# Pooled attention into a top-1 mixture of experts: another opening, and V's chunks cut at other keys

## The chip, the core and the metric

The kernel runs on one core of one Trainium2 chip. The metric is the device time of one launch in microseconds (us). A core has five engines that work beside each other: PE (TensorE, matrix products and transposes), DVE (VectorE), ACT (ScalarE), POOL (GpSimd) and SP, which here only issues transfers (DMAs).

## What is computed

Inputs are q, k and v, each of 8 batches x 8 heads x 576 rows x 64, and the weights of a gate and of 8 experts. K and V are averaged over groups of 8 rows, so that 72 keys are left for each head. Then follows ordinary attention, and after it one expert for each token.

```python
k_p = k.reshape(B, H, 72, 8, D).mean(axis=3)      # same for v_p
scores = scale * np.matmul(q, k_p.transpose(0, 1, 3, 2))
attn = softmax(scores)
x = np.matmul(attn, v_p)                          # tokens: 4608 x 512
expert_idx = argmax(x @ w_gate)
y = relu(x @ w1[e]) @ w2[e]                       # e: the token's expert
out = gate_probability * y
```

## The kernel before

The kernel has two stages. The attention goes over 36 units of 128 tokens (`units`, the loop `for i in range(NU)`), nine for each pair of batches. After it, blocks of 256 sorted tokens go through the experts (`up` and `finish`). Every engine runs its instructions in the order in which the program writes them, so the order in the text is the order on the engine.

One unit does this on PE: `u_pt` turns the exponentials of its 8 x 72 = 576 columns (padded to 640) in five transposes of 128 (L492); `u_pv` multiplies them with the masked V (L519; L514 for the four units that join two half batches); between them `g_s` makes scores of later units in two stages (L468), `g_qt` turns q (L445), and now and then a batch's K (`k_pe`, L357 and L360), V (`v_pe`, L371 to L377) and gate products (`u_pe`, L393, L395) are prepared. `rank` (L624 on) counts the tokens of each expert for a group of four units; it waits for a chain of small VectorE steps (`away` L600, `best` L606, `onehot` L615). VectorE takes the row minimum (`g_min`, L478), ScalarE the exponentials (`g_exp`, L485), VectorE divides (`u_nrm`, L549 to L551).

The 576 pooled rows of V lie in five chunks of at most 128 partitions, head after head. Chunk c holds parts of up to three heads, from head `HS[c]` on; a mask `mk` (L145) sets the rows of other heads to zero, and `SLOTS[c]` says which of the three a product takes. So `u_pv` multiplies chunk by chunk with 146, 219, 219, 219 and 73 columns (73 for a head: 64 of V, 8 of the gate, 1 for the sum). The result lies in two banks of four heads each, so the third product is cut in two: six products, 876 columns. A product of 32-bit numbers is two instructions on PE.

From the second batch on, GpSimd pools K and V (`pool`, L327, L329, L330) while other units run; most of these steps wait for the reciprocal L550 of the unit before (`on_beat`). Three buffers `kv` take K and V in turn.

The opening stands ahead of the loop. SP issues the loads in this order: K of batch 0 in three parts, a half of q (half of its rows of every head), V of batch 0, the gate weights in five small parts, the other half of q, K of batch 1, half of q of batch 1, and later V of batch 1. Meanwhile VectorE makes constants and zeroes buffers, and PE makes 36 products of ones that nobody reads (L708, `WARM`). VectorE pools K (`pool_now`, L336 to L338), PE turns each chunk twice, once for the lower 64 partitions (L717) and once for the upper (L718), because the scores take two tokens' rows at once through `BD`, a block diagonal of K. Then come the four stages of scores of the first group (`now`, `g_s`, `g_min`, `g_exp`), V pooled in two parts, `v_pe`, `u_pe`, and V masked (`u_dve`, L401, L406). GpSimd pools K of batch 1 behind V of batch 0 (L743 holds it back) and V of batch 1 behind the masked V (L746).

Of the kernel before, what the change touches and what calls it, by code (L numbers as in the profile page):

```python
# [21 lines left out]
WARM = 36  # L22
CS = 78
UPAT = (33, 34, 35)
HS = (0, 1, 3, 5, 5)
SLOTS = ((0, 2), (0, 3), (0, 3), (0, 3), (2, 3))
# [3 lines left out]
def kernel(  # L30
# [89 lines left out]

    jp = st1[1].rearrange("p c x -> p (c x)")[:, 0:128].bitcast(I32)
# [5 lines left out]
    ones = consts.tile([128, 128], F16, name="ones")  # L127
    nc.vector.memset(ones, 1.0)
# [12 lines left out]
    for c in range(5):  # L141
        nc.gpsimd.iota(rows[:, c, :], pattern=[[-KP, 3]], base=128 * c - KP * HS[c], channel_multiplier=1,
                       allow_small_or_imprecise_dtypes=True)
# [24 lines left out]
    for j, x in enumerate((0.0, 3.0, 2.0, 0.0)):  # L168
        nc.vector.memset(ahead[:, j:j + 1], x)
        nc.vector.tensor_copy(lists[:, j], inds)  # L170
    rank0 = consts.tile([128, E], F32, name="rank0")
    nc.vector.tensor_scalar(rank0, inds, float(8 * SEG + 1), None, op0=OP.mult)
    nc.vector.memset(rank0[:, 0:1], -float(1 << 17))
# [16 lines left out]
    nc.vector.tensor_scalar(head, tv, 0.0, None, op0=OP.is_equal)  # L190
# [8 lines left out]
    kv0 = consts.tile([128, 5, POOL * D], F32, name="kv0")  # L199
# [5 lines left out]
    nc.vector.tensor_scalar(thr[0:1, :], thr[0:1, :], -1.0, None, op0=OP.add)  # L205
# [35 lines left out]
    def load_kv(b, src):  # L241
        dst = kv[(2 * b + (src is vf)) % 3]
        nc.sync.dma_start(dst[0:64, 4, :], src[b, 512:576, :])
        step = 2 if b == 0 else 4
        for c in range(4 - step, -1, -step):
            nc.sync.dma_start(dst[:, c:c + step, :],
                              src[b, 128 * c:128 * (c + step), :].rearrange("(c p) x -> p c x", p=128))

# [9 lines left out]
    def load_qh(b, r):  # L258
        nc.sync.dma_start(qt[b][:, :, r:r + 2, :],
                          q[b, :, 0:128 * NM, :].rearrange("h (p r) d -> p h r d", r=NM)[:, :, r:r + 2, :])  # L260

    load_kv(0, kf)
    load_qh(0, 0)
    load_kv(0, vf)
# [3 lines left out]
    load_qh(0, 2)  # L268
    load_kv(1, kf)
    load_qh(1, 0)  # L270

    nc.vector.memset(kv[0][64:128, 4, :], 0.0)
    for i in range(1, 3):
        nc.gpsimd.memset(kv[i][64:128, 4, :], 0.0)
    nc.vector.memset(BD[0], 0.0)
# [56 lines left out]
    def pool_now(src, dst, part):  # L332
        p1 = pbig[:, 0:1280].rearrange("p (c x) -> p c x", c=5)
        p2 = pbig[:, 1280:1920].rearrange("p (c x) -> p c x", c=5)
        c = (slice(2, 5), slice(0, 2))[part]
        nc.vector.tensor_tensor(p1[:, c], src[:, c, 0:4 * D], src[:, c, 4 * D:], op=OP.add)  # L336
        nc.vector.tensor_tensor(p2[:, c], p1[:, c, 0:2 * D], p1[:, c, 2 * D:], op=OP.add)
        nc.vector.tensor_tensor(dst[:, c], p2[:, c, 0:D], p2[:, c, D:], op=OP.add)  # L338
# [58 lines left out]
    def u_dve(b):  # L397
        pm, vp = KVS.pop(("pu", b)), KVS.pop(("vp", b))

        def gates():  # L400
            nc.vector.tensor_tensor(VB[b % 3][:, :, :, D:D + E], pm[:, 0:120].rearrange("p (c s e) -> p c s e", s=3, e=E),  # L401
                                    mk[:, :, :, None].to_broadcast([128, 5, 3, E]), op=OP.mult)

        def masked(lo, hi):
            n = hi - lo
            nc.vector.tensor_tensor(VB[b % 3][:, lo:hi, :, 0:D], vp[:, lo:hi, None, :].to_broadcast([128, n, 3, D]),  # L406
                                    mk[:, lo:hi, :, None].to_broadcast([128, n, 3, D]), op=OP.mult)
            if hi == 5:
                laid.add(b)

        def masked_low():
            masked(0, 3)

        def masked_high():
            masked(3, 5)

        fillers[0:0] = [(-1, False, f) for f in (gates, masked_low, masked_high)]
# [70 lines left out]
    def u_pt(i):  # L488
        p = pbuf[i % 4]
        pp = psA.tile([128, 1024], F32, name="pp")  # L490
        for c in range(5):
            nc.tensor.transpose(pp[:, c * 128:(c + 1) * 128], p[:, c * 128:(c + 1) * 128], ident)  # L492
        pt = work.tile([128, 640], F32, name="pt")
        nc.scalar.activation(pt, pp[:, 0:640], AF.Copy)  # L494
        PP_[i] = pt

    def u_pv(i):
        b, r = units[i]
        a = PP_.pop(i)
        assert {b, b + (r is None)} <= laid and all(m[2] > b + (r is None) for m in moves)  # L500
        po = psA.tile([128, 2, 512], F32, name="po")
        PO_[i] = po
        first = {}
        for c in range(5):
            h0, hend = HS[c] + SLOTS[c][0], HS[c] + SLOTS[c][1]
            while h0 < hend:
                half = h0 // 4
                h1 = min(hend, 4 * half + 4)
                sl = slice(h0 - HS[c], h1 - HS[c])
                cols = slice((h0 - 4 * half) * CW, (h1 - 4 * half) * CW)  # L510
                st = first.get(half, True)
                if r is None:
                    for s in range(2):
                        nc.tensor.matmul(po[64 * s:64 * s + 64, half, cols],  # L514
                                         a[:, c * 128 + 64 * s:c * 128 + 64 * s + 64],
                                         VB[(b + s) % 3][:, c, sl, 0:CW], start=st, stop=False,
                                         skip_group_check=True)
                else:
                    nc.tensor.matmul(po[:, half, cols], a[:, c * 128:(c + 1) * 128],  # L519
                                     VB[b % 3][:, c, sl, 0:CW], start=st, stop=False, skip_group_check=True)  # L520
                first[half] = False
                h0 = h1
# [13 lines left out]
    def u_nrm(i, also=None):  # L536
        gidx, u = GOF[i]
        gs = bounds[gidx][1]
        if u == 0:
            drain(gidx - 2)  # L540
            flush(99, gidx - (3 if i < 30 else 2))
            X = XR[:, i % 12:i % 12 + gs, :]
            L = work.tile([128, 6, E], F32, name="L", bufs=2)
            GRP[gidx] = (X, L)
        X, L = GRP[gidx]
        po = PO_.pop(i)
        pv = po[:, :, 0:4 * CW].rearrange("p a (h x) -> p a h x", x=CW)
# [27 lines left out]
    whole(running(0), cum[:, :, None])  # L575
# [121 lines left out]
    def now(G, j):  # L697
        g_s(G, j)
        g_min(G, j)
        g_exp(G, j)  # L700

    def pooled(n, b):
        KVS[n, b] = work.tile([128, 5, D], F32, name=n, bufs=2)
        return kv[(2 * b + (n == "vp")) % 3], KVS[n, b]

# [3 lines left out]
    src, kp = pooled("kp", 0)  # L709
    pool_now(src, kp, 0)  # L710
    pool_now(src, kp, 1)
    g_qt(0, 0)
    g_qt(0, 1)
    pm = psA.tile([128, 1024], F32, name="pp")
    for c in (4, 2, 3, 0, 1):
        n = 128 if c < 4 else 64
        nc.tensor.transpose(pm[0:64, c * 128:c * 128 + n], kp[0:n, c], ident[0:n, 0:n])  # L717
        nc.tensor.matmul(pm[64:128, c * 128:c * 128 + n], kp[0:n, c], ident[0:n, 0:n], start=True, stop=True)  # L718
    for s in range(2):
        nc.scalar.activation(half(0, s), pm[64 * s:64 * s + 64, 0:H * KP], AF.Copy, scale=-SC)  # L720
    src, vp = pooled("vp", 0)
    pool_now(src, vp, 0)
    now(0, 0)
    pool_now(src, vp, 1)
    g_s(0, 1)
    v_pe(0)
    v_act(0)
    g_min(0, 1)
    g_exp(0, 1)
    g_s(0, 2)  # L730
    g_min(0, 2)
    g_exp(0, 2)
    u_pe(0)
    g_s(0, 3)
    g_min(0, 3)
    g_exp(0, 3)
    u_dve(0)
    drain(0)
    load_kv(1, vf)
    load_qh(1, 2)  # L740
    load_kv(2, kf)
    load_ql(0)
    nc.gpsimd.tensor_tensor(spacer[:, 0:1], vp[0:1, 0, 0:1], zf[0:1], op=OP.add)  # L743
    pool_k(1, 0)
    pool_k(1, 1)
    nc.gpsimd.tensor_tensor(spacer[:, 0:1], VB[0][0:1, 0, 0, 0:1], zf[0:1], op=OP.add)  # L746
    pool_v(1, 0)
    pool_v(1, 1)
    g_qt(1, 0)
# [3 lines left out]
    g_min(1, 1)  # L753
    load_kv(2, vf)
# [17 lines left out]
    prep(1, (0, ""), (1, ""), (2, ""))  # L772
# [164 lines left out]
    for i in range(NU):  # L937
# [8 lines left out]
        u_pt(i)  # L946
# [353 lines left out]
```

## Time and profile before

| | us |
|---|---|
| median of 3 runs | 611.68 (611.6 to 613.2) |
| the profiled execution | 610.65 |
| its span, from the first to the last instruction | 608.6 |
| PE busy | 581.4 (96% of the span) |
| first `u_pt` of the loop | 28.20 |
| last `u_pt` of the loop | 187.96 |

The profiled execution spends 2.05 us outside its span. PE is busy nearly throughout; VectorE 50%, ScalarE 45%, GpSimd 43% over the whole span, and more than that during the attention.

### The profile page before, as it was taken

To read this page: it belongs to the slowest core of one execution; us is meant where nothing else is said; L and a number is where in the kernel's file an instruction comes from. 1 tells how busy PE (TensorE), PEld (TensorE's weight loads), DVE (VectorE), ACT (ScalarE), POOL (GpSimd) and SP (SyncE) were. 2 spreads that over 40 slices of the span, in tenths; PEclk is the share of its full clock that TensorE was granted. 3 is DMA by queue.
4 is the path that set the end of the run, shared out by engine and by line. 5 is a ranking of instruction groups with operands and counts; after the bars stand their busy time and mean duration, and the time that the engine had idled before them with its cause. 6 is when DMAs were issued, how large, how long until landed. Compare 5 with 4: busy or idle time off the path is not lost. (4 is left out here: it accounts for less than half of the span.)

```text
span 608.6 us, 15118 instructions
## 1 busy us (share of the span) xinstructions
PE 581.4 (96%) x4391; PEld 436.9 (72%) x4392; DVE 304.0 (50%) x618; ACT 274.8 (45%) x620; POOL 263.1 (43%) x476
## 2 busy tenths in 40 slices
PE   6799999999799999999999999999999999999994
PEld 4699999898799467667756766757767567667672
DVE  5357778879865645214623212273123722183683
ACT  1577687877662245214522212272222722172671
POOL 5675888789964514202321121313222221214265
PEclk9999999999799999999999999999999999999998
DMA  9996789973345795985592143328543192318320
GB/s 246 301 318 203 259 249 328 326 233 136 117 114 191 192 350 128 406 237 108 136 323 66 54 108 83 83 55 284 153 108 81 35 355 81 102 34 291 90 59 11
DMA packets 96256, 107.10 MB, mean 176 GB/s; under 512 B 54366, under 2 KB 64606, under 8 KB 96224
## 3 DMA queue, kind: packets, MB, share of 16 engines
q1 hardware_dynamic: 89584, 85.72, 48.9%
q0 software_dynamic: 6640, 20.99, 9.1%
q8 instruction: 16, 0.26, 0.2%
q14 instruction: 16, 0.13, 0.1%
HBM read 72.99 MB, written 23.37 MB: 158 GB/s over the span
## 5 line engine op out<-in xcount | busy, mean ns | idle before, releaser
L998 PEld LDWEIGHTS <-bd 128*128 128x128 f16 x936 | 91.2, 98 | 105.8 <-DVE bd L992 0.9
L992 DVE SCALAR_TENSOR_TENSOR bd<-ps,bd 128x512 f16<-128x512 f32 (+1 forms) x44 | 27.5, 630 | 144.1 <-ACT bd L988 144.0
L1208 POOL TENSOR_TENSOR spacer<-ql,iG 1x1 f32<-1x1 f32 x44 | 18.6, 422 | 162.8 <-ACT ql L1204 153.0
L485 ACT ACTIVATE both<-ps,nmx 128x72 f32<-128x72 f32 x288 | 69.8, 347 | 7.1 <-DVE nmx L478 7.0
L519 PE MATMUL po<-vb,pt 128*128 128x146 f32 (+2 forms) x384 | 61.1, 308 | 1.5 <-DVE both L551 1.3
L519 PEld LDWEIGHTS po<-vb,pt 128*128 128x128 f32 x384 | 57.5, 192 | 4.0 <-issue 1.7
L998 PE MATMUL po<-w,bd 128*128 128x512 f16 x264 | 59.2, 379 | 0.0
L998 PE MATMUL po<-kv,bd 128*128 128x512 f16 x264 | 58.8, 379 | 0.0
L1209 POOL DMA_INDIRECT out_dram<-ql,iG x44 | 47.1, 1071 | 22.0 <-issue 20.6
L988 ACT ACTIVATE bd<-ps 128x512 f16<-128x512 f32 (+1 forms) x44 | 23.8, 547 | 69.1 <-PE L924 55.5
L468 PE MATMUL ps<-bd,qT 128*128 128x144 f32 x256 | 47.5, 313 | 2.1 <-ACT bd L720 1.4
L998 PE MATMUL pq<-kv,bd 128*128 128x512 f16 x216 | 48.1, 379 | 0.0
L653 POOL DMA_INDIRECT x_by_expert<-both,rpos x36 | 36.3, 1009 | 23.1 <-DVE both L649 10.1
L327 POOL TENSOR_TENSOR st<-kv 128x1280 f32<-128x1280 f32 x14 | 40.6, 2897 | 12.1 <-DVE ri L550 9.6
L926 PE MATMUL ps<-kv,qt 128*128 128x256 f16 (+1 forms) x176 | 44.8, 263 | 0.9 <-DVE qt L113 0.9
L924 PE MATMUL ps<-kv,w 128*128 128x256 f16 (+1 forms) x176 | 43.1, 258 | 1.9 <-ACT kv L111 1.5
L924 PE MATMUL ps<-kv,qt 128*128 128x256 f16 (+1 forms) x176 | 44.8, 263 | 0.0
L925 PE MATMUL ps<-kv,qt 128*128 128x256 f16 (+1 forms) x176 | 44.8, 263 | 0.0
L494 ACT ACTIVATE pt<-pp 128x640 f32<-128x640 f32 x36 | 25.5, 708 | 41.8 <-PE pp L492 41.8
L926 PE MATMUL ps<-kv,w 128*128 128x256 f16 (+1 forms) x176 | 43.1, 258 | 0.0
L925 PE MATMUL ps<-kv,w 128*128 128x256 f16 (+1 forms) x176 | 43.1, 258 | 0.0
L998 PE MATMUL pq<-w,bd 128*128 128x512 f16 x192 | 42.7, 379 | 0.0
(236 smaller groups left out, 1284.4 us busy)
## 6 DMA issues: line engine op xcount, KB each, us to landing
st<-in_moe_w_dram SPq DMA_DIRECT2D x8, 2048.0 KB, 13.7
both<-in_moe_w_dram SPq DMA_DIRECT2D x6, 2048.0 KB, 12.7
vb<-x_by_expert SPq DMA_DIRECT2D x16, 578.0 KB, 4.4
kv<-in_k_dram SPq DMA_DIRECT2D x7, 1024.0 KB, 9.0
kv<-in_v_dram SPq DMA_DIRECT2D x7, 1024.0 KB, 11.4
qt<-in_q_dram SPq DMA_DIRECT2D x6, 1024.0 KB, 11.5
st<-in_moe_w_dram SPq DMA_DIRECT2D x4, 1024.0 KB, 7.1
qt<-in_q_dram SPq DMA_DIRECT2D x4, 512.0 KB, 7.1
```

Source lines behind the costliest of these rows:

```text
L327: on_beat(nc.gpsimd.tensor_tensor(t1, src[:, :, 0:4 * D], src[:, :, 4 * D:], op=OP.add))
L468: nc.tensor.matmul(ps[:, x * 2 * KP:(x + 1) * 2 * KP], t[:, h, :], BD[b % 3][:, :, h, :], start=True, stop=True)
L485: nc.scalar.activation(p[:, h * KP:(h + 1) * KP], ps[:, x * KP:(x + 1) * KP], AF.Exp, bias=nmx[:, x:x + 1], scale=-1.0)
L494: nc.scalar.activation(pt, pp[:, 0:640], AF.Copy)
L519: nc.tensor.matmul(po[:, half, cols], a[:, c * 128:(c + 1) * 128], VB[b % 3][:, c, sl, 0:CW], start=st, stop=False, skip_group_check=True)
L653: st = nc.gpsimd.indirect_dma_start(out=xs, out_offset=bass.IndirectOffsetOnAxis(ap=Z["pos"][:, u:u + 1], axis=0), in_=X[:, u, :], in_offs ...
L924: nc.tensor.matmul(dst, wh, xT[:, d, 0:n], start=(d == 0), stop=False)
L925: nc.tensor.matmul(dst, wh, xT[:, DC + d, 0:n], start=False, stop=False)
L926: nc.tensor.matmul(dst, wl, xT[:, d, 0:n], start=False, stop=(d == DC - 1))
L992: V.scalar_tensor_tensor(l, p, 0.0, h, op0=OP.max, op1=OP.subtract)
L998: nc.tensor.matmul(y, hT[x][:, f, 128 * j:128 * j + 128], W2[s][z][:, f, :], start=(half == x == z == f == 0), stop=(half == z == 1 and f ...
L1209: st = nc.gpsimd.indirect_dma_start(out=out, out_offset=bass.IndirectOffsetOnAxis(ap=iG[:, j:j + 1], axis=0), in_=ys[j], in_offset=None, b ...
```

## The change

- V's chunks begin at keys 0, 128, 216, 344 and 472 (`VK`) instead of every 128. Chunks overlap, the last holds 104 rows. With `HS` and `SLOTS` as in the diff the products have 146, 146, 146, 219 and 146 columns, and the result lies in one run of eight heads whose border between banks falls between heads 2 and 3: five products, 803 columns. V's loads become three transfers of 616 rows in place of two of 576. `masked` lays out two heads instead of three for the first three chunks.
- In the opening, pooled K is written twice side by side (`kp` with 2 x 64 columns), so that one transpose serves lower and upper partitions (`k_first`); pooling, turning and copying of K go in two parts (chunks 0 and 1, then 2 to 4). V goes in the same two parts.
- The first q is loaded by heads (four and four, all rows) ahead of V, the second q in one transfer.
- 68 unread products instead of 36. The ones are set first on VectorE; small constants move behind the opening (`constants`); one zeroing moves from VectorE to GpSimd.
- The first `u_pt` goes into the opening, K of batch 1 is turned behind the first `u_pv` instead of ahead of it, V's and the gate's steps of batch 1 one unit later.

```diff
-WARM = 36
+WARM = 68
-HS = (0, 1, 3, 5, 5)
-SLOTS = ((0, 2), (0, 3), (0, 3), (0, 3), (2, 3))
+VK = (0, 128, 216, 344, 472)
+HS = (0, 1, 3, 4, 5)
+SLOTS = ((0, 2), (0, 2), (0, 2), (0, 3), (1, 3))
+LEFT = 3
...
     def load_kv(b, src):
         dst = kv[(2 * b + (src is vf)) % 3]
-        nc.sync.dma_start(dst[0:64, 4, :], src[b, 512:576, :])
+        if src is vf:
+            for c in (0, 2):
+                nc.sync.dma_start(dst[:, c:c + 2, :],
+                                  src[b, VK[c]:VK[c] + 256, :].rearrange("(c p) x -> p c x", p=128))
+            nc.sync.dma_start(dst[0:S - VK[4], 4, :], src[b, VK[4]:S, :])
+            return
...
     load_kv(0, kf)
     load_qh(0, 0)
+    load_qh(0, 4)
     load_kv(0, vf)
...
-    load_qh(0, 2)
     load_kv(1, kf)
-    load_qh(1, 0)
-
-    nc.vector.memset(kv[0][64:128, 4, :], 0.0)
...
+    load_q(1)
+    nc.gpsimd.memset(BD[0], 0.0)
...
         for c in range(5):
-            nc.tensor.transpose(pp[:, c * 128:(c + 1) * 128], p[:, c * 128:(c + 1) * 128], ident)
+            nc.tensor.transpose(pp[:, c * 128:(c + 1) * 128], p[:, VK[c]:VK[c] + 128], ident)
...
+            sl = slice(*SLOTS[c])
+            h = HS[c] + SLOTS[c][0]
+            cols = slice(o0 + h * CW, o0 + (HS[c] + SLOTS[c][1]) * CW)
...
+                nc.tensor.matmul(po[:, cols], a[:, c * 128:(c + 1) * 128], VB[b % 3][:, c, sl, 0:CW],
+                                 start=h in (0, LEFT), stop=False, skip_group_check=True)
...
+    def k_first(cs):
+        for c in cs:
+            n = 128 if c < 4 else 64
+            nc.tensor.transpose(pm[:, c * 128:c * 128 + n], kp[0:n, c].rearrange("p a d -> p (a d)"), ident[0:n, 0:n])
+
+    def k_keep(s, lo, hi):
+        if s and lo:
+            nc.vector.tensor_scalar(half(0, s)[:, lo:hi], pm[64:128, lo:hi], -SC, None, op0=OP.mult)
+        else:
+            nc.scalar.activation(half(0, s)[:, lo:hi], pm[64 * s:64 * s + 64, lo:hi], AF.Copy, scale=-SC)
+
+    pool_now(kv[0], kp, slice(0, 2))
+    k_first((0, 1))
+    k_keep(0, 0, 256)
+    k_keep(1, 0, 256)
+    pool_now(kv[0], kp, slice(2, 5))
     g_qt(0, 0)
+    k_first((2, 3, 4))
+    k_keep(0, 256, 576)
+    k_keep(1, 256, 576)
     g_qt(0, 1)
     now(0, 0)
+    now(0, 1)
+    pool_now(kv[1], vp, slice(0, 2))
+    g_qt(1, 0)
+    gates, masked = u_dve(0)
+    now(0, 2)
+    masked(0, 2)
+    pool_now(kv[1], vp, slice(2, 5))
+    now(0, 3)
+    u_pt(0)
     v_pe(0)
     v_act(0)
     u_pe(0)
+    masked(2, 3)
+    masked(3, 5)
+    gates()
     load_kv(1, vf)
-    load_qh(1, 2)
     load_kv(2, kf)
     load_ql(0)
...
-    g_qt(1, 0)
     g_qt(1, 1)
     now(1, 0)
     g_s(1, 1)
     g_min(1, 1)
+    constants()
     load_kv(2, vf)
...
-    prep(1, (0, ""), (1, ""), (2, ""))
+    prep(1, (0, "2"), (2, ""), (3, ""))
...
-        u_pt(i)
+        if i:
+            u_pt(i)
```

## Rows read from the trace of the kernel before

**Rows 1.** The page, part 1: busy time, share and instructions of each engine.

```profile
PE 581.4 (96%) x4391; PEld 436.9 (72%) x4392; DVE 304.0 (50%) x618; ACT 274.8 (45%) x620; POOL 263.1 (43%) x476
```

**Rows 2.** Windows, opening: length, PE, PEld, DVE, ACT, POOL busy, clock, DMA share, GB/s.

```profile
5.70:9.00 3.30, 0.00 (x0) 0.00 (x0) 3.20 (x7) 0.00 (x0) 3.30 (x6) 1.00 1.06 275
```

**Rows 3.** Timeline, opening, PE: start, us, what; idle before and its releaser in brackets.

```profile
1.67 3.76 PEld L708 LDWEIGHTS <-ones 128*128 128x128 f16 x36 [1.35 <-DVE ones L128]
9.05 1.97 PE L445 MATMUL pq<-ident,qt 128*128 128x128 f32 x8 [3.35 <-DMA qt<-in_q_dram]
...
23.31 0.98 PEld L468 LDWEIGHTS ps<-bd,qT 128*128 128x128 f32 x4
...
32.18 1.76 PEld L519 LDWEIGHTS po<-vb,pt 128*128 128x128 f32 x12 [0.17 <-issue]
33.86 0.55 PEld L468 LDWEIGHTS ps<-bd,qT 128*128 128x128 f32 x4
```

**Rows 4.** DMA view of the first 40 us: GB/s in slices of 1 us.

```profile
GB/s 0 0 199 303 399 337 288 334 203 320 380 221 221 276 220 299 377 324 332 262 215 350 386 333 299 203 258 389 354 150 246 238 379 383 225 293 360 381 353 348
```

**Rows 5.** Timeline, opening, VectorE and ScalarE.

```profile
11.00 0.96 DVE L336 TENSOR_TENSOR st<-kv 128x768 f32<-128x768 f32 x1 [1.61 <-DMA kv<-in_v_dram]
18.79 0.96 ACT L485 ACTIVATE both<-ps,nmx 128x72 f32<-128x72 f32 x4 [1.91 <-DVE nmx L478]
20.06 0.45 DVE L478 TENSOR_REDUCE nmx<-ps 128x4 f32<-128x288 f32 x1
```

**Rows 6.** Timeline, GpSimd: pooling of batch 1's K and V and of batch 2's K.

```profile
20.37 2.88 POOL L327 TENSOR_TENSOR st<-kv 128x1280 f32<-128x1280 f32 x1
...
26.50 0.43 POOL L746 TENSOR_TENSOR spacer<-vb,zf 1x1 f32<-1x1 f32 x1 [0.69 <-DVE vb L406]
26.90 2.87 POOL L327 TENSOR_TENSOR st<-kv 128x1280 f32<-128x1280 f32 x1
...
36.88 0.86 POOL L330 TENSOR_TENSOR kp<-st 128x320 f32<-128x320 f32 x1
```

**Rows 7.** Timeline, PE, in the third unit: gate products, K of batch 2, next unit's scores.

```profile
40.44 0.53 PEld L393 LDWEIGHTS pq<-wgb,vT 128*128 128x128 f32 x4
42.99 0.44 PEld L357 LDWEIGHTS pq<-ident,kp 128*64 128x64 f32 x4
```

**Rows 8.** Timeline, PE, narrow windows inside one `u_pv`; each line begins with its first matmul.

```profile
37.15 0.53 PE L519 MATMUL po<-vb,pt 128*128 128x219 f32 x2
37.33 0.52 PE L519 MATMUL po<-vb,pt 128*128 128x219 f32 x3
37.52 0.51 PE L519 MATMUL po<-vb,pt 128*128 128x73 f32 x3
37.58 0.57 PE L519 MATMUL po<-vb,pt 128*128 128x73 f32 x3
```

**Rows 9.** Timeline, GpSimd, VectorE and PE around units 24 and 28.

```profile
141.41 0.19 PE L624 MATMUL pq<-oh,before 128*128 128x32 f16 x1 [1.24 <-DVE oh L615]
157.03 1.91 POOL L118 TENSOR_TENSOR kv<-st,swc 128x1024 f32<-128x1024 f32 x1
157.11 1.89 DVE L600 TENSOR_TENSOR ra<-L,rm 128x32 f32<-128x32 f32 x1
159.03 2.16 DVE L606 SCALAR_TENSOR_TENSOR req<-ra,down 128x32 f32<-128x32 f32 x1
161.69 0.18 PE L624 MATMUL pq<-oh,before 128*128 128x32 f16 x1 [3.36 <-DVE oh L615]
161.83 1.31 PE L468 MATMUL ps<-bd,qT 128*128 128x144 f32 x4
168.43 0.70 PE L468 MATMUL ps<-bd,qT 128*128 128x144 f32 x4
172.28 0.70 PE L468 MATMUL ps<-bd,qT 128*128 128x144 f32 x4
```

**Rows 10.** Windows of 5 us, columns as in rows 2: the stretch of that wait.

```profile
160.00:165.00 5.00, 3.31 (x19) 3.29 (x19) 3.63 (x10) 0.91 (x3) 4.81 (x5) 0.60 0.28 82
```

More of the change, by code (lines that the diff above doesn't have):

```diff
@@ L204, with constants @@
     nc.gpsimd.iota(thr, pattern=[[SEG, E]], base=0, channel_multiplier=BLK, allow_small_or_imprecise_dtypes=True)
-    nc.vector.tensor_scalar(thr[0:1, :], thr[0:1, :], -1.0, None, op0=OP.add)
+    def constants():
+        for j, x in enumerate((0.0, 3.0, 2.0, 0.0)):
+            nc.vector.memset(ahead[:, j:j + 1], x)
+            nc.vector.tensor_copy(lists[:, j], inds)
+        nc.vector.tensor_scalar(rank0, inds, float(8 * SEG + 1), None, op0=OP.mult)
+        nc.vector.memset(rank0[:, 0:1], -float(1 << 17))
+        nc.vector.tensor_scalar(head, tv, 0.0, None, op0=OP.is_equal)
+        nc.vector.tensor_scalar(thr[0:1, :], thr[0:1, :], -1.0, None, op0=OP.add)
+        whole(running(0), cum[:, :, None])
     loads = ctx.enter_context(tc.tile_pool(name="loads", bufs=1))
@@ L242, in load_kv @@
         dst = kv[(2 * b + (src is vf)) % 3]
[L243 removed]
+        if src is vf:
[4 more added lines that the diff above has]
+            return
         step = 2 if b == 0 else 4
[L245 removed]
+        for c in range(0, 4, step):
             nc.sync.dma_start(dst[:, c:c + step, :],
                               src[b, 128 * c:128 * (c + step), :].rearrange("(c p) x -> p c x", p=128))
+        nc.sync.dma_start(dst[0:64, 4, :], src[b, 512:576, :])
     def load_q(b):
@@ L415, in masked_high @@
             masked(3, 5)
+        if b == 0:
+            return gates, masked
         fillers[0:0] = [(-1, False, f) for f in (gates, masked_low, masked_high)]
@@ L500, in u_pv @@
         assert {b, b + (r is None)} <= laid and all(m[2] > b + (r is None) for m in moves)
-        po = psA.tile([128, 2, 512], F32, name="po")
-        PO_[i] = po
-        first = {}
+        po = psA.tile([128, 2, 512], F32, name="po").rearrange("p a x -> p (a x)")
+        o0 = 512 - LEFT * CW
+        PO_[i] = po[:, o0:o0 + H * CW]
         for c in range(5):
[L505 to L522, printed above, removed]
+            sl = slice(*SLOTS[c])
+            h = HS[c] + SLOTS[c][0]
+            cols = slice(o0 + h * CW, o0 + (HS[c] + SLOTS[c][1]) * CW)
+            if r is None:
+                for s in range(2):
+                    nc.tensor.matmul(po[64 * s:64 * s + 64, cols], a[:, c * 128 + 64 * s:c * 128 + 64 * s + 64],
+                                     VB[(b + s) % 3][:, c, sl, 0:CW], start=h in (0, LEFT), stop=False,
+                                     skip_group_check=True)
+            else:
+                nc.tensor.matmul(po[:, cols], a[:, c * 128:(c + 1) * 128], VB[b % 3][:, c, sl, 0:CW],
+                                 start=h in (0, LEFT), stop=False, skip_group_check=True)
     GRP = {}
@@ L713 @@
     g_qt(0, 1)
[L714 to L722, printed above, removed]
```

81 lines of the change are left out of this document (31 added, 50 removed).

## The prediction

> **What bounds the kernel now.** I read the page's busy times first, then the opening, then the places where PE waits. PE is busy 96% of the span [rows 1], so work taken from PE counts wherever nothing else is late. The exception is the opening. From 5.70 to 9.00 PE does nothing while the transfers run flat out [rows 2], then it waits 3.35 us for q [rows 3]. In the opening PE is also at the lower of its two clock levels, although the window's clock column reads 1.00. Four instructions of scores take 0.98 us at 23.31 and 0.55 us at 33.86 [rows 3]. 36 products of 128 columns take 3.76 us, 0.104 us each [rows 3], which is 128 columns at 1.2 GHz. So the spacing of like instructions is the witness here. The 36 products did not raise the clock in this execution; what came behind them still ran at half speed.
>
> In the attention PE runs dense, except that it waits at `rank` for VectorE. The worst wait is 3.36 us at 161.69 [rows 9]. There `away` (L600) and `best` (L606), which are small, take 1.89 and 2.16 us because GpSimd's L118 starts 0.08 us ahead of L600 and L119 follows. In that stretch the granted clock is 0.60 in the mean [rows 10], between the levels of 2.4 GHz (1.00) and 1.2 GHz (0.50): it fell after the idle time. And the next unit takes 168.43 - 161.83 = 6.60 us where the one after it takes 3.85 [rows 9].
>
> **Part 1, the opening.** I price it at one point, the turn of batch 2's K in the third unit, at 42.99 before [rows 7], because there GpSimd's pooling meets PE.
>
> Data first. I add up the slices of the DMA view [rows 4]. By 7.5 us 1.70 MB have come, which is K (1.18) and half of q (0.52); q was used at 9.05 [rows 3], a lag of 1.5. By 9.9 us 2.36 MB have come, which adds V's first parts; VectorE used them at 11.00 [rows 5], a lag of 1.1. I take 1.3. Behind the change the order is K 1.18, q 1.05, V 1.26 (616 rows of 2 KB), K of batch 1 1.18, q 1.05, V of batch 1 1.26, in all 6.98 MB against 6.29 up to the same V. The slices reach 6.98 MB at 25.5 us, so it lands near 26.8. q now moves in pieces of 1 KB instead of 512 bytes. If that removes the three weak slices (203, 221, 221), some 0.2 MB or 0.8 us are won: 26.0. At the best stretch's pace it would be 24.5.
>
> GpSimd pools that V from 26.90 and has batch 2's K at 36.88 + 0.86 = 37.74 [rows 6], so 10.84 us later. Before, its start hung on the masked V at 26.50 [rows 6]; now it hangs on the data. That chain gives 36.8 to 37.6, at best 35.3. So the faster opening buys GpSimd almost nothing; the wait for the masked V becomes a wait for a transfer.
>
> PE's own way there. The second half of q is complete at 2.23 MB, 9.5 + 1.3 = 10.8 us. The four stages of scores need 0.96 us of ScalarE each and a minimum of 0.45 [rows 5]. The last minimum stands on VectorE behind V's second pooling, whose data (3.49 MB) land at 14.0 + 1.3 = 15.3. Its first step alone is 0.96 [rows 5], the next two halve the columns, so some 1.8: 17.1. Then 0.45 and 0.96: 18.5. Between there and the first `u_pv` PE has 16 turns at 0.11 (0.44 for four [rows 7]), three stages of scores at 0.55 [rows 3] and the gate products (from 40.44 [rows 7] to the next product at 41.35: 0.9): 4.35 us at 2.4 GHz, twice that at 1.2, and some 2 us in which it waits for ScalarE's copies and exponentials. So the first `u_pv` begins between 24.9 and 29.2, against 32.18 [rows 3]. From there to the turn of batch 2's K took 42.99 - 32.18 = 10.8. The change puts 12 turns of batch 1's K in (1.3), takes the gate products out (0.9) and shortens three products (0.4): 10.8 again. That gives 35.7 to 40.0.
>
> The later of both ways counts: 37.2, the middle of GpSimd's chain, since PE's lower end is ahead of it. 42.99 - 37.2 = 5.8; before, the gate products of batch 1 were done by then (0.9), so **4.9 us** are won. Bounds: PE at 1.2 GHz throughout gives 2.1; the best pace of transfers gives 6.3. The single transpose in place of two, the constants moved behind (some 2 us of VectorE, in the way only of the second group's minimum) and the zeroing on GpSimd (1 us where GpSimd is idle for batch 0's data) I cost at nothing beyond this: the data cover them. If the data came at once, the turns would be worth about 2 us.
>
> The 68 products end, at 0.104 each from about 1.1 us on, at 8.2 us or sooner if the clock rises in between; the first pooled chunks are ready near 6.6. So they can delay the first turns by up to 1.6 us, but q's first half arrives at 8.8 anyway, and the delay is covered. Whether the clock, once up, lasts is open, since PE would then idle from about 14.6 to 18.5. After 3.4 us of idle it was down at 161.83; after 1.24 us at 141.41 nothing slowed [rows 9]. So I expect it down again by the first `u_pt`, which is why I don't take the lower end. The Trainium skill, TensorE: Matmul & The Clock Gate, Part 4 (PE-mode transpose), speaks against the change too: transposes, it says, don't count as busy for the clock. By that rule the turns behind the 68 products would not hold the clock, and the time would be that of the 1.2 GHz end, 2.8 us later. The half-speed turns from 9.05 on agree, but don't prove it.
>
> **Part 2, the products with V.** In one unit 876 columns take 33.86 - 32.18 = 1.68 us [rows 3] in 12 instructions. The change turns 2 x 146, 2 x 219, 2 x 73 into 4 x 146, 1 x 219, every product two instructions. By columns alone it saves 73 / 876 of 1.68 = 0.14. By spacing, 219 columns take 0.18 and 73 take 0.06 [rows 8], up to 0.11 where a heavier one follows; 146 take as long as the scores' 144, 0.55 / 4 = 0.138 [rows 3]. So the change is 2 x 0.18 + 4 x (0.06 to 0.11) - 4 x 0.138 = 0.05 to 0.25. I take **0.14**, inside both. 33 units behind the opening's point: 4.6 us. PE is dense there, so it lies on the path, save where PE waits for VectorE behind GpSimd: the wait of 1.24 us at 141.41 [rows 9] just grows by what units 22 to 24 save, 0.4. **4.2 us** remain (1.2 to 7.8). Two extra SP issues for each V and 7% more of V's bytes are behind work that is loaded units ahead: nothing. VectorE's shorter masks are off the path.
>
> **Sum.** 610.65 (span 608.6 and 2.05 around it) - 4.9 - 4.2 = 601.55. The median of the runs lies 1.03 above the profiled execution: **602.5**. The experts' stage only moves earlier.
>
> **Rivals.**
> - *The wait at 161.69 dissolves.* Without the lock L606 would begin at 157.11 + 0.25 + 0.03 = 157.39 (0.25 being my estimate of a free L600). Units 25 to 27 bring VectorE 3 x 0.14 = 0.42 forward, while GpSimd, which is all but never idle there (4.81 of 5 us [rows 10]), stays: 156.97, 0.06 ahead of L118 at 157.03. Then only `onehot` is caught, until 158.94, and PE goes on at 159.2 instead of 161.69, without the slow unit: 2.5 + 2.75 = 5.2 us. That gives 597.3. Against it: the margin is thinner than the scatter of one instruction. The Trainium skill, SBUF, names the lock: one pair of ports between VectorE and GpSimd, held for a whole instruction; 1.89 us for L600 against GpSimd's 1.91 agrees.
> - *The opening gives only its lower end, 2.1,* with PE slow from the idle time on: 605.3.
> - *The products don't shrink as their columns do,* at 0.05 a unit (weight loads or issue set the pace): 33 x 0.05 less the same 0.4 at unit 24: 605.5.
> - *Slower.* `rank` comes eight times, and only one wait now costs clock. New phases between VectorE and GpSimd could catch two more groups as at unit 28, at 3.36 + 2.75 = 6.1 us each: 602.5 + 12.2 = 614.7. It takes two; one gives 608.6. For it speaks that GpSimd leaves so few gaps [rows 10]; against it, that the earlier waits are 1.24 us or less and GpSimd's steps hang on the reciprocals, so the phases move together.
>
> **How the numbers follow.** Chances: forecast 0.42, dissolved wait 0.30, lower opening 0.11, small products 0.08, one more caught wait 0.04, slower 0.05. A measurement of this kernel tells about 0.3% (1.8 us) from no change. Faster 0.91, same 0.04, slower 0.05. The range 595.0 to 608.0 takes in the dissolved wait with a better opening and the weak openings with weak products.
>
> **What would show it.** GpSimd's L327 for V of batch 1 should begin at 26 to 27 behind a DMA, and K of batch 2 be turned near 37. L519 should be ten instructions in about 1.54 us. The wait at unit 28 should read 3 us or near 1. Wrong would be: GpSimd starting that V before 25 (transfers faster), the first `u_pv` behind 29, or `rank` waits above 3 us elsewhere.

## The result and the profile after

The changed kernel takes 604.29 us (median of 4 runs, 601.66 to 605.96), the kernel before 612.44 beside it; the ratio is 0.9865 with a 95% interval of 0.9837 to 0.9893. The forecast was 602.5 us with a range of 595.0 to 608.0. A repeat on another chip gave 600.87 (0.9832, 0.9799 to 0.9865). Why the two medians lie 3.4 us apart is open, but for one stall that is shown below. The execution profiled first is the slowest of its four: 605.96 us, span 603.7.

The page of after, part 1, against [rows 1]:

```profile
PE 571.7 (95%) x4333; PEld 426.4 (71%) x4334; DVE 301.5 (50%) x619; ACT 274.6 (45%) x621; POOL 265.5 (44%) x477
```

PE has 58 instructions fewer and 9.7 us less work; the span is 4.9 us shorter. PE stays the busiest engine, but it stands idle more. Where the time went is read off four marks, in us from the start of the span:

| mark | before | after | after, repeated |
|---|---|---|---|
| K of batch 2 turned (PEld) | 42.99 | 38.54 | 38.25 |
| last `u_pt` | 187.96 | 178.50 | 178.15 |
| second block of the experts | 210.25 | 204.81 | 200.22 |
| end | 608.6 | 603.7 | 599.1 |

So the opening gives 4.45, the attention 5.0 more, the passage to the experts takes 4.0 back in the first execution and nothing in the repeat, and the rest is as long as it was within 0.6 us.

The opening of after, PEld rows of the timeline (the last one stands against the last of [rows 7]):

```profile
1.07 5.88 PEld L712 LDWEIGHTS <-ones 128*128 128x128 f16 x68 [0.75 <-DVE ones L124]
25.77 2.74 PEld L531 LDWEIGHTS po<-vb,pt 128*128 128x128 f32 x10
38.54 0.45 PEld L371 LDWEIGHTS pq<-ident,kp 128*64 128x64 f32 x4
```

68 products at the pace of the 36 [rows 3], 0.104 us, would take 7.1 us; they take 5.88, so the clock rose inside them. It did not last. PE waited 2.2 us for exponentials before 17.04, and the windows (columns as in [rows 2]) show the granted clock at the lower level from 20 on:

```profile
20.00:24.00 4.00, 3.36 (x14) 2.96 (x14) 1.27 (x7) 1.59 (x6) 3.84 (x3) 0.50 1.07 344
24.00:28.00 4.00, 3.99 (x16) 3.96 (x17) 1.74 (x13) 2.35 (x9) 2.27 (x3) 0.50 1.09 262
28.00:33.00 5.00, 4.89 (x33) 4.04 (x32) 1.75 (x5) 2.24 (x6) 4.84 (x4) 0.86 1.12 277
```

The first `u_pv` at 25.77 therefore takes 2.74 us for its ten products, and PE is itself late at batch 2's K. GpSimd is as forecast: V of batch 1 begins at 26.70 behind a DMA, K of batch 2 is pooled at 36.72 + 0.86 = 37.58 (against [rows 6]):

```profile
26.70 2.89 POOL L338 TENSOR_TENSOR st<-kv 128x1280 f32<-128x1280 f32 x1 [1.73 <-DMA kv<-in_v_dram]
...
36.72 0.86 POOL L341 TENSOR_TENSOR kp<-st 128x320 f32<-128x320 f32 x1
```

A unit in the steady stretch, PE, first before, then after (one `u_pv` and the scores behind it):

```profile
63.18 1.91 PE L519 MATMUL po<-vb,pt 128*128 128x146 f32 x12
64.92 0.70 PE L468 MATMUL ps<-bd,qT 128*128 128x144 f32 x4
65.46 0.71 PE L492 MATMUL pp<-ident,both 128*128 128x128 f32 x5
```

```profile
41.87 1.64 PE L531 MATMUL po<-vb,pt 128*128 128x146 f32 x10
43.34 0.65 PE L485 MATMUL ps<-bd,qT 128*128 128x144 f32 x4
43.83 0.71 PE L509 MATMUL pp<-ident,both 128*128 128x128 f32 x5
```

From start to start `u_pv` takes 1.74 before and 1.47 after, the scores behind it 0.54 and 0.49: 0.32 us a unit. In narrow windows inside one `u_pv` of after the starts of the products of 146 columns (each line begins with the first matmul of its window) lie 0.125 us apart:

```profile
42.22 0.54 PE L531 MATMUL po<-vb,pt 128*128 128x146 f32 x3
42.35 0.54 PE L531 MATMUL po<-vb,pt 128*128 128x146 f32 x3
42.47 0.60 PE L531 MATMUL po<-vb,pt 128*128 128x146 f32 x3
42.60 0.47 PE L531 MATMUL po<-vb,pt 128*128 128x146 f32 x2
```

Before, the short products of 73 columns hold up what stands behind them. The first instruction of 146 columns behind such a pair takes 0.17 us to the next start:

```profile
64.08 0.65 PE L519 MATMUL po<-vb,pt 128*128 128x146 f32 x3
64.25 0.66 PE L519 MATMUL po<-vb,pt 128*128 128x146 f32 x3
```

The scores behind `u_pv`, which ended on such a pair, show the same: they took 0.54 and now take 0.49, or 0.12 for each instruction of 144 columns.

The other side of the account is `rank`. Before, PE waits there three times for `oh`, 4.8 us in all (the view of waits: total, times, longest); after, seven times:

```profile
PE pq L632 <- DVE oh L623: 7.8, 7, 2.2
```

Unit 24, where [rows 9] show 1.24 us, now looks as unit 28 did before (timeline of GpSimd, VectorE and PE):

```profile
129.53 1.90 POOL L120 TENSOR_TENSOR kv<-st,swc 128x1024 f32<-128x1024 f32 x1
131.51 2.12 POOL L121 TENSOR_TENSOR w<-kv,w 128x1024 f16<-128x1024 f32 x1
130.57 0.92 DVE L608 TENSOR_TENSOR ra<-L,rm 128x32 f32<-128x32 f32 x1
131.53 2.15 DVE L614 SCALAR_TENSOR_TENSOR req<-ra,down 128x32 f32<-128x32 f32 x1
134.18 0.19 PE L632 MATMUL pq<-oh,before 128*128 128x32 f16 x1 [2.19 <-DVE oh L623]
135.69 1.17 PE L485 MATMUL ps<-bd,qT 128*128 128x144 f32 x4
```

The window around it, its clock in the third column from the right:

```profile
130.00:140.00 10.00, 7.81 (x52) 7.08 (x51) 8.65 (x21) 6.28 (x25) 9.44 (x8) 0.83 0.48 160
```

GpSimd's L121 starts 0.02 us ahead of `best` (L614) and both end within 0.05 us of each other; PE loses 2.19 us and from 135.69 on runs scores at half pace. At unit 28 the wait is 1.99, in other executions up to 4.24.

The loss in the passage to the experts, in the first execution alone, in PE's timeline and in the window:

```profile
200.29 0.38 PE L1137 MATMUL pq<-ident,tf 128*8 128x128 f32 x1 [2.58 <-DVE tab L1134]
```

```profile
198.00:204.00 6.00, 3.71 (x11) 1.43 (x12) 2.67 (x9) 0.69 (x1) 4.10 (x10) 0.72 0.30 108
```

In each of the thirteen other profiled executions, the kernel before among them, PE waits 0.44 to 0.46 us at this turn. So nothing ties the 2.58 us to the change.

### The profile page after: what moved, and what is told of

It reads as the page before. It is cut to its first block, busy times and chain, and to the rows that moved or that the text cites. A ratio compares the mean times of both kernels' runs of the same rounds, so it can differ in the third digit from the quotient of the medians.

```text
span 603.7 us, 15016 instructions
## 1 busy us (share of the span) xinstructions
PE 571.7 (95%) x4333; PEld 426.4 (71%) x4334; DVE 301.5 (50%) x619; ACT 274.6 (45%) x621; POOL 265.5 (44%) x477
## 5 line engine op out<-in xcount | busy, mean ns | idle before, releaser
L1013 PE MATMUL po<-w,bd 128*128 128x512 f16 x264 | 60.5, 386 | 0.0
L531 PE MATMUL po<-vb,pt 128*128 128x146 f32 (+1 forms) x320 | 52.7, 311 | 1.8 <-ACT pt L511 1.8
L531 PEld LDWEIGHTS po<-vb,pt 128*128 128x128 f32 x320 | 47.1, 194 | 3.7 <-ACT pt L511 2.9
L485 PE MATMUL ps<-bd,qT 128*128 128x144 f32 x256 | 45.6, 304 | 1.4 <-ACT both L502 1.2
L338 POOL TENSOR_TENSOR st<-kv 128x1280 f32<-128x1280 f32 x14 | 40.6, 2903 | 11.8 <-DVE ri L559 7.1
```

Source lines behind the costliest of these rows:

```text
L338: on_beat(nc.gpsimd.tensor_tensor(t1, src[:, :, 0:4 * D], src[:, :, 4 * D:], op=OP.add))
L485: nc.tensor.matmul(ps[:, x * 2 * KP:(x + 1) * 2 * KP], t[:, h, :], BD[b % 3][:, :, h, :], start=True, stop=True)
L531: nc.tensor.matmul(po[:, cols], a[:, c * 128:(c + 1) * 128], VB[b % 3][:, c, sl, 0:CW], start=h in (0, LEFT), stop=False, skip_group_check ...
L1013: nc.tensor.matmul(y, hT[x][:, f, 128 * j:128 * j + 128], W2[s][z][:, f, :], start=(half == x == z == f == 0), stop=(half == z == 1 and f ...
```

## The experiments

The theory to be tested was that three things set the time: GpSimd's pooling sets the end of the opening, shorter products shorten each unit, and small steps of VectorE that stand beside GpSimd's long ones take part of it back. Marks are those of the table above, from one profiled execution each; each kernel also ran against the kernel before, on its own chip.

| kernel | median us (lowest to highest) | ratio to before | K of batch 2 | last `u_pt` | second block |
|---|---|---|---|---|---|
| again | 600.87 (600.55 to 601.44) | 0.9832 | 38.25 | 178.15 | 200.22 |
| opening_only | 609.69 (604.68 to 612.72) | 0.9987 | 37.16 | 181.65 | 203.86 |
| products_only | 606.51 (605.08 to 608.95) | 0.9930 | 40.65 | 178.77 | 200.90 |
| warm36 | 603.00 (601.63 to 603.55) | 0.9858 | 39.56 | 179.55 | 201.65 |
| rank_later | 607.29 (605.69 to 608.89) | 0.9938 | 38.50 | 185.79 | 207.86 |
| no_split | 592.30 (591.50 to 592.92) | 0.9696 | 38.29 | 168.98 | 191.11 |
| more_warm | 600.07 (599.17 to 600.31) | 0.9815 | 37.20 | 177.85 | 199.99 |
| split_quarters | 601.49 (599.52 to 602.88) | 0.9845 | 37.62 | 177.10 | 199.21 |
| opening_no_split | 603.22 (599.26 to 607.08) | 0.9861 | 39.08 | 177.43 | 199.70 |
| before_no_split | 603.91 (603.36 to 603.95) | 0.9874 | 44.25 | 181.22 | 203.56 |
| split_behind | 599.04 (597.62 to 600.63) | 0.9806 | 38.23 | 175.97 | 198.09 |
| split_pool_behind | 603.28 (601.87 to 604.89) | 0.9867 | 37.88 | 181.48 | 203.55 |

**The parts of the change, one at a time** (four kernels on one chip).

`again`, the changed kernel unaltered:

> The changed kernel once more, unaltered. Its first profile lost 4.0 us between the last turn of a unit and the second block of experts (a gain of 9.5 us at the one point, 5.4 at the other). If that loss belongs to the change, it is here again, with PE idle some 2.6 us ahead of the turn of the table. If it belongs to the one execution, the gain of some 9 us at the last unit reaches the end, and the time is nearer 602 than 606.

`opening_only`, the old products and chunks put back:

```diff
-VK = (0, 128, 216, 344, 472)
-HS = (0, 1, 3, 4, 5)
-SLOTS = ((0, 2), (0, 2), (0, 2), (0, 3), (1, 3))
-LEFT = 3
+VK = (0, 128, 256, 384, 512)
+HS = (0, 1, 3, 5, 5)
+SLOTS = ((0, 2), (0, 3), (0, 3), (0, 3), (2, 3))
...
```

> The changed kernel with the products of before: chunks every 128 keys, six products, 876 columns, two banks of four heads. My theory: opening and products add up, and the opening is worth what was won at the turn of batch 2's K, 42.99 - 38.54 less 0.9 of gate products = 3.5 us: about 609. Rival: the opening is the whole gain and the columns are hidden: about 604.

`products_only`, the kernel before with the new chunks and products alone:

> The kernel before with V's chunks at the new keys and five products of 803 columns (V in three transfers, first V in the old order), and the old opening. My theory: a unit's products fall from 1.68 to 1.48 us, 36 x 0.20 = 7.2 us, of which the waits at rank take back 1 to 3: 606 to 608. Rival: the columns are hidden behind VectorE or the transfers: 611 to 612.

`warm36`:

```diff
-WARM = 68
+WARM = 36
```

> The changed kernel with 36 unread products instead of 68. My theory: the clock stays at 1.2 GHz until some 30 us, so the first scores and turns run at half pace, but transfers and ScalarE set most of that stretch, and GpSimd has batch 2's K no earlier than 37.5 anyway: its turn comes 0 to 2 us later than 38.54, the time is 604 to 606. Rival: the raised clock makes the opening's gain: 607 to 608.

Measured up to the second block in the profiled executions, the opening alone gives 6.4 us, the products alone 9.35, both 10.0. They don't add up in these executions, and the waits at `rank` show where it goes. The view of waits, first of opening_only, then of products_only, then of again:

```profile
PE pq L639 <- DVE oh L630: 5.2, 4, 3.4
```

```profile
PE pq L626 <- DVE oh L617: 9.8, 7, 4.2
```

```profile
PE pq L632 <- DVE oh L623: 9.2, 7, 3.3
```

With the old products the waits are nearly the old ones; with the new products there are seven, with either opening. Of the 2.4 us by which again has K of batch 2 earlier than products_only, 0.9 are the gate products that stand behind the mark in again and ahead of it in products_only. At the end of the wait of unit 24 1.3 us are left (134.04 against 135.31). Both executions waited 2.2 us there, but in products_only the scores ran on at full pace:

```profile
135.31 0.19 PE L626 MATMUL pq<-oh,before 128*128 128x32 f16 x1 [2.16 <-DVE oh L617]
135.44 0.74 PE L478 MATMUL ps<-bd,qT 128*128 128x144 f32 x4
```

In again the same four take 1.31 us at 134.18. Then again waits 3.29 us at unit 28 and products_only 4.22, and they leave it at 154.87 and 155.49: PE reaches this wait sooner or later, and its end moves by little (153.69 in more_warm).

The opening_only execution ran its scores at full pace from 24.35 on and turned K of batch 2 at 37.16, where the forecast had put it. It is also the fastest of ten that spread over 8 us. That execution is the 604 of the rival, the median the 609 of the theory. By the medians the picture is another one: the opening alone gives 0.6 us (its interval, 0.9956 to 1.0019, takes in no gain at all), the products alone 3.8, both 9.5. So what the opening is worth by itself in time is open; no profile shows the slower runs of opening_only.

36 products in place of 68 cost 2.1 us, and the runs of the two don't overlap. The 603.0 of warm36 lie under its forecast of 604 to 606: the clock did not stay down until 30 us. The view of windows has it at 0.93 from 14 to 18, 0.50 from 18 to 24 and 0.95 from 24 to 30.

Behind the second block the products_only execution took 402.5 us where again took 398.9. PE's timeline shows 3.1 of the 3.6 us: PE stood for 1.5 us, and 15 of the products behind that came every 0.21 us in place of 0.11:

```profile
266.48 0.27 PE L926 MATMUL ps<-kv,qt 128*128 128x256 f16 x1 [1.50 <-issue]
```

opening_no_split has the like at 286.81 (2.22 us, for `w` of VectorE), the first execution of after at 200.29. Whether the longer runs of opening_only have such stalls is open too.

**Does the clock or GpSimd end the opening?** `more_warm`:

```diff
     now(0, 3)
+    for _ in range(44):
+        nc.tensor.matmul(warm[:, 0, 0:128], ones, ones, start=True, stop=True)
     u_pt(0)
```

> The changed kernel with 44 more unread products between the last scores of the opening and the first u_pt, where PE stood idle and the clock had fallen by 20 us. Theory: GpSimd's pooling (V of batch 1 from 26.7, K of batch 2 done at 37.6) sets the opening, so the first u_pv comes 1 to 2 us earlier at full clock, batch 2's K is turned at 37.6 to 38 instead of 38.4, and the time falls by 0 to 1 us: 600 to 601. Rival: PE's clock sets the opening: batch 2's K is turned near 36.5 and the time falls by 2 us or more: 598.5 or less. If the 44 products stand in the way of u_pt (they end behind its exponentials), it comes later and the time rises by up to 1 us.

PE and GpSimd in more_warm:

```profile
23.63 1.53 PE L531 MATMUL po<-vb,pt 128*128 128x146 f32 x10
37.20 0.63 PE L371 MATMUL pq<-ident,kp 128*64 128x128 f32 x4 [2.38 <-POOL kp L341]
36.29 0.86 POOL L341 TENSOR_TENSOR kp<-st 128x320 f32<-128x320 f32 x1
```

The clock now lasts, the first `u_pv` comes 2.7 us earlier than in again and runs at full pace, and PE reaches batch 2's K at 34.8 and waits 2.38 us for GpSimd. So GpSimd's chain is the floor, and after's PE was 1 us above it because of its clock. The 1.05 us won on again at that mark are 0.3 at the last `u_pt`; the wait at unit 28 grew to 4.24. The time is 0.8 us under again's, on another chip; by their ratios (0.9775 to 0.9855 and 0.9799 to 0.9865) the two can't be told apart, as the theory had it.

**What makes PE wait at `rank`?** `rank_later` puts the one-hot transposes behind the next unit's scores:

```diff
-        if (i, "pe") not in hooks:
+        if i < 30 or (i, "pe") not in hooks:
             fill_pe()
...
         run(i, "pe2")
-        fill_pe()
+        if i > 28:
+            fill_pe()
```

> The changed kernel, with rank (the transposes of the one-hot rows) put behind the next unit's u_pt and first scores instead of ahead of them; nothing is computed otherwise. Theory: in all kernels with the new products PE stands at rank at every group (0.6, 0.9, 1.0, 0.7, 0.5, 2.2 and 2.0 to 4.2 us in the profiled executions so far, 8 to 11 us in all, and at half clock for a unit behind each of the two long ones), because away, best and onehot are held up behind GpSimd's long instructions. With about 2 us of other PE work put ahead of rank, the waits up to 2.2 us go, and the last shrinks to 1 to 2 us; the clock stays up. Gain 5 to 9 us on the changed kernel: 592 to 596. Rival: something else of VectorE (nmx, the reciprocals) is then late by the same amount, and the waits only move to the next unit's scores or u_pv: 599 to 602.

The forecast of 592 to 596 was missed. The rival holds, and more than that: it is 6.4 us slower than again. One unit of it (VectorE, ScalarE, PE):

```profile
118.68 2.89 DVE L608 TENSOR_TENSOR ra<-L,rm 128x32 f32<-128x32 f32 x1
123.26 0.81 DVE L495 TENSOR_REDUCE nmx<-ps 128x4 f32<-128x288 f32 x2
123.74 0.96 ACT L502 ACTIVATE both<-ps,nmx 128x72 f32<-128x72 f32 x4 [1.32 <-DVE nmx L495]
124.57 0.61 ACT L465 ACTIVATE qT<-pq 128x512 f32<-128x512 f32 x1
125.24 1.09 PE L407 MATMUL pq<-wgb,vT 128*128 128x48 f32 x4 [2.59 <-ACT qT L465]
```

`away` stands 2.89 us beside GpSimd's pooling, the minimum of the scores is queued behind it, then the exponentials, then q's copy on ScalarE, then PE. VectorE's queue is blocked, and whoever needs it next waits. Why the sum is worse than before, and not only moved, these rows don't show.

`no_split`:

```diff
-            beat(nc.gpsimd.tensor_tensor(t, src, sw.to_broadcast(list(src.shape)), op=OP.mult))
-            nc.gpsimd.tensor_tensor(l, t, h, op=OP.subtract)
+            beat(nc.gpsimd.memset(l, 0.0))
```

> The changed kernel, where GpSimd's two instructions for the weights it splits (L120 and L121, 2.1 us each beside VectorE) become one that zeroes the low half; the low halves of those weights (5 of 8 parts of the first expert) are left out. Theory: the two long waits at rank (2.2 us near 134, 2.0 to 4.2 near 155) come from these instructions standing beside away and best, so they fall to 1 us or less and the half-clock stretches behind them go: 3 + 2.5 or so, 594 to 598. The waits near 48 to 116, where only the pooling (L338) stands beside them, stay at 0.5 to 1.0. Rival: GpSimd's pooling, which then runs earlier, catches the same two groups: waits there stay at 2 us or more and the time at 600 to 602.

VectorE's timeline around unit 24 in no_split, then the window of 25 us, first of no_split, then of again:

```profile
130.07 0.18 DVE L607 TENSOR_TENSOR ra<-L,rm 128x32 f32<-128x32 f32 x1
130.29 0.19 DVE L613 SCALAR_TENSOR_TENSOR req<-ra,down 128x32 f32<-128x32 f32 x1
```

```profile
120.00:145.00 25.00, 25.00 (x216) 23.31 (x215) 20.32 (x63) 21.25 (x70) 17.28 (x23) 1.00 0.72 230
```

```profile
120.00:145.00 25.00, 22.82 (x184) 21.05 (x183) 20.54 (x55) 17.70 (x60) 21.82 (x18) 0.93 0.61 191
```

`best` takes 0.19 us where it took 2.15, PE has no idle time and the clock stays at 1.00. The last `u_pt` comes 9.2 us earlier and the kernel takes 8.6 us less, more than was expected: the two long waits with their slow stretches were worth more than the opening. The kernel leaves out work, so this is what the splits cost and not a gain that can be kept. The waits near 65 to 116 stay (0.55 to 1.05), beside the pooling of L338; in split_pool_behind below, which moves that pooling, they are gone.

`split_quarters` cuts each of the two instructions into four of 256 columns:

```diff
-            beat(nc.gpsimd.tensor_tensor(t, src, sw.to_broadcast(list(src.shape)), op=OP.mult))
-            nc.gpsimd.tensor_tensor(l, t, h, op=OP.subtract)
...
+            for p in parts:
+                ins = nc.gpsimd.tensor_tensor(t[p], src[p], swc[:, 0:1].to_broadcast([128, 256]), op=OP.mult)
...
+            for p in parts:
+                nc.gpsimd.tensor_tensor(l[p], t[p], h[p], op=OP.subtract)
```

> The changed kernel, in which each of GpSimd's two instructions for a part of the weights (L120 and L121, 128x1024, 1.9 and 2.1 us) is cut into four of 256 columns; all of it is computed. Theory: a small instruction of VectorE that meets one is held for 0.5 us in place of 2.1, so best takes 0.7 at the most where it took 2.15, the waits of 2.2 and 3.3 us at rank near 134 and 155 fall to 1 us or less, and the clock stays up: 594 to 597 us. Rival: GpSimd's four parts follow each other so closely that VectorE gets no turn in between, and away and best wait as long as before: 599 to 602. Second rival: cutting makes GpSimd so much slower (over 0.3 us for each cut) that the constants of the next stage are late: 600 or more with a new wait behind 178.

GpSimd and VectorE at unit 24:

```profile
128.61 2.32 POOL L126 TENSOR_TENSOR kv<-st,swc 128x256 f32<-128x256 f32 x4
130.89 2.53 POOL L131 TENSOR_TENSOR w<-kv,w 128x256 f16<-128x256 f32 x4
129.64 3.21 DVE L618 TENSOR_TENSOR ra<-L,rm 128x32 f32<-128x32 f32 x1
```

The first rival holds. `away` is held from 129.64 to 132.85, across the ends of several of GpSimd's instructions that follow each other without a pause. The waits at `rank` are 2.91 us there and 2.34 at unit 28. So shorter instructions do not let VectorE in at the next end. It came in at 132.85 all the same, where GpSimd's rows show no pause until 133.42; why at this point and not at an earlier end is open. A kernel that cuts the pooling as well has no time, so nothing is said of it.

`split_behind` lets the splits of units 24 and 28 wait for VectorE's last small step of the group; `split_pool_behind` does the same with the first pooling of K in a group's first unit:

```diff
-            V.tensor_tensor(Z["oh"], Z["eq"][:, 0:gs], Z["m2"][:, 0:gs].to_broadcast(sh), op=OP.is_equal)
+            beat.append(V.tensor_tensor(Z["oh"], Z["eq"][:, 0:gs], Z["m2"][:, 0:gs].to_broadcast(sh), op=OP.is_equal))
...
-        put(at, "q", wsplit, 0, j, "p", 0, on_beat)
+        put(at, "pe2" if at % 4 == 0 else "q", wsplit, 0, j, "p", 0, on_beat)
...
-                        put(POOLAT[b] + x + y, "q", f, b, y)
+                        put(POOLAT[b] + x + y, "q" if x + y or not POOLAT[b] else "pe2", f, b, y)
```

The last pair of lines is split_pool_behind's alone; VectorE's own splits go into `beat` like `onehot`.

> The changed kernel, all of it computed, in which the two of GpSimd's weight splits that fall into a unit that begins a group (units 24 and 28) are issued behind onehot of that unit and wait for VectorE's last small step, in place of the reciprocals one unit before. Theory: the long waits at rank come from the split standing beside away and best, and VectorE gets no turn until GpSimd pauses. With GpSimd started some 2 us later, away and best take 0.2 us each, the waits of 2.2 and 3.3 us near 134 and 155 go, as they do without the splits, and the clock stays up; GpSimd has those 4 us before its last scatters. 592 to 595. Rival: the delay of 2 us in each moves later splits beside away and best of another group, or the first expert's weights come late: a new wait of 2 us or more, 597 to 601.

> As split_behind, and the first step of the pooling of K that begins in a group's first unit (batches 3 to 7) behind onehot as well. Theory: the waits of 0.6 to 1.0 us at rank near 65, 82, 99 and 116 have L338 beside away and go: 2.5 to 3 us less than split_behind, 589 to 592. Rival: GpSimd, which is busy for some 15 of 17 us of a batch there, is then late with K: a wait for a pooled chunk takes their place, and the time is that of split_behind or 1 to 3 us above it.

In split_behind the long waits at units 24 and 28 are gone, and V's masking on VectorE (L421, two instructions) is caught by the splits in their place; PE then waits for `u_nrm` behind it (timeline, then waits):

```profile
142.28 4.78 DVE L421 TENSOR_TENSOR vb<-vp,mk 128x384 f32<-128x384 f32 x2
142.32 1.90 POOL L120 TENSOR_TENSOR kv<-st,swc 128x1024 f32<-128x1024 f32 x1
144.30 2.34 POOL L121 TENSOR_TENSOR w<-kv,w 128x1024 f16<-128x1024 f32 x1
```

```profile
PE po L531 <- DVE both L560: 4.5, 2, 3.1
```

In split_pool_behind PE waits for `u_nrm` in six units, V's masking takes 1.22 us an instruction in the median (0.55 in again), one wait of 0.5 us is left at `rank`, and the first expert's inputs are late:

```profile
PE po L531 <- DVE both L560: 9.9, 6, 2.9
PE ps L938 <- DMA kv<-bd: 2.6, 1, 2.6
```

So 599.04, the rival's time, and 603.28, 4.2 above it where the rival had 1 to 3. split_behind has the lowest median after no_split, but its ratio (0.9764 to 0.9847) can't be told from again's. In these kernels the place of the splits decides who waits; only leaving them out removed the cost. Another engine for them was not tried.

**The parts without the splits.** `before_no_split` and `opening_no_split` are the kernel before and opening_only with the edit of no_split.

> The kernel before, with GpSimd's two instructions for the weights replaced by one that zeroes the low half (the same low halves are left out). Theory: of its waits at rank, 3.36 us at unit 28 goes with the slow unit behind it (6.1 us in all), and 1.24 at unit 24: 602 to 604 against 610 to 611 for the kernel before. Rival: the pooling takes the splits' place beside away and best, and the time falls by 2 us or less.

> The new opening with the old products and old chunks of keys, and GpSimd's two instructions for the weights replaced by one that zeroes the low half (the low halves of 5 of the first expert's 8 parts are left out). With before_no_split it gives the opening's own worth without the long waits at rank. Theory: opening and products add up once those waits are out: with 592.3 for both parts, some 4 us for the opening and 6.5 (0.2 us for each of 33 units) for the products: opening_no_split 598 to 599, before_no_split 602 to 603, and the runs of each lie within 2 us of each other. Rival: they don't add up for another reason (VectorE is late everywhere): opening_no_split is within 1 us of before_no_split.

Up to the second block, 203.56, 199.70 and 191.11 (no_split): the opening gives 3.9 and the products 8.6. The kernel before takes 6.7 us less without the splits (610.61 beside it), as its theory had it, the changed one 8.6 less. opening_no_split missed its forecast of 598 to 599: its runs spread over 8 us, and the profiled one has the stall at 286.81 and some 3.7 us more behind the second block than again. By the medians the opening gives 0.7 there and the products 10.9 (no_split ran on another chip), so the opening's own worth in time is as open as in opening_only. Of the products' 8.6 us, 0.8 stand at K of batch 2 already; the other 7.8 go with 33 units at 0.32, 10.6, less the 2.8 us by which PE waits longer at `rank` in no_split (3.4 against 0.6), waits elsewhere left aside.

## Why the prediction was right, point by point

- **The opening, 4.9.** It gave 4.45 less 0.9 for the gate products that now stand behind the mark: 3.5. GpSimd's chain came out at 37.58 (forecast 36.8 to 37.6), the V at 26.70 (26 to 27), the first `u_pv` at 25.77 (24.9 to 29.2). The step that failed is "37.2, the middle of GpSimd's chain, since PE's lower end is ahead of it". The text itself expected the clock down by the first `u_pt`, which made PE's upper half, 37.9 to 40.0, the later of both ways; PE arrived at 38.54. The first `u_pv` was early, but from there to the mark PE took 12.8 us and not the 10.8 of the text, since that stretch began at the lower clock (2.74 us for the first ten products). more_warm, with the clock up, arrived at 37.20.
- **The 68 products.** They raised the clock inside them, which the 36 of [rows 3] had not done, and the idle time after the scores took it down again, as expected. In warm36 36 products took 3.44 us, so the clock rose near their end, but at PE's next work it was down: four turns of q at 7.93 took 0.72 us, in again 0.42 at 8.23. The 68 are worth 2.1 us. That the turns behind them would let the clock fall was not seen: until the wait that ends at 17.04, turns and scores ran at full pace; turns alone were not tested.
- **The products, 0.14 us a unit.** 0.32 were measured, beyond the upper bound of 0.25. Two terms were mis-sized or missing. The new instruction of 146 columns was priced at 0.138, the duration of a group of four scores over four; their starts stand 0.12 apart, and those of 146 columns inside `u_pv` 0.125. For the four new instructions that is 0.05. And what stands behind a short pair of 73 columns lost 0.05, twice a unit: once inside `u_pv`, once in the scores behind it. The change removes both short pairs, 0.10 in all, and no term had it. The rest is within the rounding of the text's own sum, whose middle is 0.15. The 1.68 us are PEld's rows; PE's rows give 1.74 for a unit. The sign of 1.54 us for the ten instructions was missed with them: 1.35 on the same rows (41.87 to 43.22).
- **What VectorE takes back, 0.4.** Too small. 33 units at 0.32 would be 10.6; the attention won 5.9 (5.0 and the 0.9 above). Waits at `rank` rose from 4.8 to 7.8 us (9.2 in again), two more of 1.23 and 0.53 for `pt` came where one of 1.27 for VectorE had been (in again only 0.2), and a slow stretch was added at unit 24. The wait there grew by 0.95 and not by 0.4. The forecast had only unit 24's wait grow by what units 22 to 24 save; no_split, which has five waits at `rank` where before_no_split has one of 0.2, shows that PE, once faster, runs into VectorE at most groups even without the splits. The two errors, products too small and waits too small, nearly cancel: 4.2 against 5.9.
- **The rivals.** The wait at 161.69 did not dissolve: it is 1.99, 3.29 or 4.24 in the executions profiled. The slower side came half true: one more group, unit 24, was caught with 2.2 us and a slow stretch. Its cause was the one named, GpSimd beside `away` and `best`. No wait over 3 us stood elsewhere.
- **"The experts' stage only moves earlier."** So it nearly did in the repeat (398.9 us behind the second block, 398.35 before). In the first execution 4.0 us went in the passage before it.
- **The median 1.03 above the profiled execution.** Here it lies 1.67 below.

In sum the total is near partly by luck: the mechanisms were the right ones, but the opening gave 1.4 us less than forecast and the attention 1.7 more, and within the attention two sizes were off in opposite directions.

## What to carry to other kernels

When PE gets faster per unit, look first at the engine pair that feeds it: here the waits for VectorE and the slow stretches behind them took back 4.7 of the 10.6 us that the products won by the estimate above, and moving the work around among queues only chose another victim, while leaving GpSimd's splits out gave 8.6 us. Price a product by the distance between starts of its like, not by the duration of a group, and count what it does to the instruction behind it. An opening that ends on two chains needs the later one under the clock that you expect, not under the one you hope for.

## What the runs showed of the hardware beyond the forecast

A small step of VectorE can be held over several instructions of GpSimd in a row: 3.21 us in split_quarters, with parts of 0.6 to 0.7 us, and it came in where GpSimd's rows show no pause. And idle time of one length has not one price in clock. At unit 24 PE stood for 2.15 to 2.19 us in five profiled executions of the new products. Behind it the granted clock from 130 to 140 is 0.83 in after and again, and 1.00 in products_only, more_warm and warm36.
